# A decayed-attention and two-layer kernel on one core: the opening's running state summed in PSUM, longer warming matmuls, and a new order of the opening

## Chip, core and metric

One core of a Trainium2 chip runs the whole kernel. The metric is device time in microseconds, from the median of three runs. Engines are called as in the profile: PE (TensorE matmuls), PEld (its weight loads), DVE (VectorE), ACT (ScalarE), POOL (GpSimd), SP (SyncE, which issues the DMAs).

## What is computed

Decayed linear attention without a softmax, over 4 sequences of 576 positions with 8 heads of 64, and then two feed-forward layers with different activations, all in float32 and to float32 accuracy:

```python
scores = scale * np.matmul(q, k.transpose(0, 1, 3, 2))
Dmat = np.where(rel >= 0, gamma[:, None, None] ** rel[None, :, :], 0.0)
x = np.matmul(scores * Dmat[None], v)              # -> (2304, 512), heads side by side
h = x @ w_in;   x = (h * np.cos(h)) @ w_out        # 512 -> 2048 -> 512
h = x @ w2_in;  out = np.where(h >= 1, h, np.where(h <= -1, 0, (h + 1)**2 / 4)) @ w2_out
```

The decay is a power of a constant per head, so that attention can go chunk by chunk: within a chunk by masked scores, and across chunks by a running state, a 64x64 matrix per head, which is multiplied by the head's decay over the chunk and gets the sum of k times v of the chunk added.

## The kernel before

**Layout.** The 2304 positions are cut into blocks of 256, 512, 512, 512 and 512 for the first layer (`BLOCKS`), and the sequences into chunks of 128 or 64 that don't cross a block. Chunks 0 to 10 belong to the first three blocks (chunk 4 is the last of the first sequence, 9 the last of the second, 10 begins the third; 4 and 6 have 64 positions). A float32 operand of a large matmul is split into a high and a low part, and three matmuls make a product. A weight comes as float64 and is converted to such a pair by five steps on ACT and DVE, named X, C, W, O and M; the layer's input weight c is wi c, the output weight wo c. Converted wi tiles are also stored to DRAM for the later blocks. From c = 4 on a raw weight is loaded twice, into `raw` and `rsh`.

**A chunk's steps.** `load:qk`, `load:kv`; `q` and `k` scale q and k by tables of decay powers, on the engine that the letter behind them names (V DVE, G POOL, A ACT); `scores`; `masked` (two products with the mask table, on DVE); `state`, the matmuls of k with v; `add_state`, which makes the new state T; `across` and `attend`, the matmuls with the old state T and with the masked scores; `high` and `low`, which split the result for the first layer. `copied` copies the result out of PSUM first; then low runs on POOL instead of DVE. The `state` of every chunk goes to fresh PSUM banks y2 and y3 (`start` on its first matmuls). `add_state` (lines 374 to 386) then makes T: for a sequence's first chunk two copies on ACT, else four DVE operations of 64 columns each, old T times a decay plus the banks. The decays are columns 12 to 19 of `ktb`, a table of 20 columns, and k's are columns 0 to 11.

**First layer.** A slot is a block and an inner column tile c of 128. Its steps are m (12 matmuls, first product), h, a, A, b, C, g, G (copy and activation on ACT, DVE, POOL) and M (12 matmuls, second product). m:0 and m:1 belong to block 0 with wi0 and wi1, m:2 to block 1 with wi0, m:3 to block 0 with wi2, m:4 to block 1 with wi1, m:5 to block 0 with wi3, m:7 with wi4.

**Order.** The opening, attention for chunks 0 to 10, the first conversions and slots 0 to 7, is written out by hand: `OPENING` (lines 64 to 81) is a list of steps, `take` issues them, and what an engine gets stands in that order on it, the DMA issues of SP among them. Behind it the loop over slots goes on with the same step functions, and a scheduler orders the rest. `load_raw` of the remaining weights follows the list, so on SP they stand behind the list's last store, that of wi4. Steps `warm:n` are matmuls of a zero tile `wz` into a PSUM tile that nobody reads:

```python
wz = const.tile([P, P], BF16, tag="wz", name="wz")
m = PE.matmul(wt[:, 0:P], wz, wz, start=True, stop=True)
warm(20)
```

Of the kernel before, what the change touches and what calls it, by code (L numbers as in the profile page):

```python
# [63 lines left out]
OPENING = """
load:kv0 load:kt load:qk0 load:qt load:qk1 load:mt load:kv1 load:qk2 load:wi0 load:kv2 load:qk3 load:kv3 load:qk4
load:wo0 load:qk5 load:kv4 load:kv5 load:wi1 load:kv6 load:qk6 k:0V state:0 add_state:0 q:0V warm:5 scores:0 q:1V
warm:1 scores:1 masked:0 across:1 masked:1 attend:0 k:1G load:qk7 load:kv7 attend:1 high:0 q:2G low:0 state:1 copied:1
load:qk8 load:kv8 add_state:1 scores:2 X:wi0 high:1 W:wi0 across:2 k:2V O:wi0 C:wi0 warm:4 state:2 q:3V k:3A
add_state:2 low:1 warm:4 scores:3 masked:2 across:3 q:4G masked:3 X:wo0 warm:1 state:3 attend:2 M:wi0 store:0
load:qk10 attend:3 q:5G add_state:3 high:2 load:qk9 load:wi2 load:kv9 load:kv10 load:wo1 low:2 m:0 copied:3 W:wo0 k:5A  # L70
scores:4 C:wo0 scores:5 across:4 X:wi1 masked:4 k:6G state:5 masked:5 attend:4 add_state:5 q:6G high:4 state:6 C:wi1
attend:5 O:wo0 high:3 low:4 q:7G high:5 add_state:6 warm:1 scores:6 across:6 h:0 low:3 low:5 a:0 k:7A masked:6 warm:2
scores:7 A:0 M:wo0 across:7 attend:6 load:wi3 masked:7 q:8G high:6 state:7 k:8A low:6 attend:7 q:10G add_state:7
scores:8 W:wi1 high:7 state:8 M:wi1 across:8 O:wi1 store:1 load:wo2 low:7 q:9G b:0 warm:1 m:1 add_state:8 X:wi2 C:0
scores:9 h:1 C:wi2 g:0 across:9 a:1 m:2 A:1 W:wi2 b:1 masked:9 k:10G O:wi2 X:wo1 masked:8 G:0 state:10 h:2 attend:9
a:2 C:1 M:wi2 store:2 g:1 load:wi4 attend:8 high:9 W:wo1 X:wi3 m:3 G:1 low:9 add_state:10 W:wi3 O:wo1 m:4 h:3 C:wo1
a:3 O:wi3 C:wi3 high:8 A:2 M:0 h:4 low:8 b:2 A:3 scores:10 M:wo1 b:3 load:wo3 C:2 M:1 a:4 C:3 g:2 A:4 X:wo2 M:wi3
store:3 b:4 G:2 masked:10 m:5 g:3 C:4 attend:10 h:5 G:3 a:5 g:4 m:6 A:5 high:10 C:wo2 b:5 G:4 low:10 X:wi4 M:2 h:6 C:5
a:6 W:wo2 M:wo2 O:wo2 A:6 X:wo3 M:3 W:wi4 b:6 W:wo3 O:wi4 M:4 C:6 O:wo3 C:wi4 g:6 M:wi4 store:4 g:5 C:wo3 m:7 M:wo3
G:5 h:7 a:7 G:6 M:5 A:7 M:6 b:7 C:7 g:7 G:7  # L80
"""
# [949 lines left out]
```

## Time and profile before

| | |
|---|---|
| time, median of 3 runs | 861.61 us (859.78 to 862.84) |
| the profiled execution's own time | 860.27 us |
| its span | 858.5 us |
| PE busy | 834.2 us (97%), 5719 matmuls |
| DVE busy | 582.5 us (68%) |
| ACT busy | 443.4 us (52%) |
| POOL busy | 137.5 us (16%) |

The profiled execution took 1.34 us less than the median. The span is what the trace covers; 1.8 us lie around it. Busy times are of the whole span. The stages differ: attention and the opening up to about 80 us, conversion of the first layer's weights beside its matmuls up to about 160, and then matmuls alone. Times in the rows are counted from the span's start. A group's line number is that of a helper (L102) for everything in the opening.

### The profile page before, as it was taken

The numbers are of one execution on the slowest core, as the hardware profiler recorded it, in microseconds if no ns is written. First come the engines' busy times: TensorE is split into PE (matmuls) and PEld (weight loads), VectorE is DVE, ScalarE is ACT, GpSimd is POOL, SyncE is SP. The second block draws the span as 40 slices with busy tenths as digits, with TensorE's granted clock in tenths as the row PEclk, the third lists the DMA queues.
The fourth block names the chain that finished last, engine by engine and source line by source line (L and its number), as shares of the span: only waits on it lengthen the run. The fifth ranks groups of instructions, "written<-read, shape, count | busy, mean of one in ns | idle before, by whom it ended". The sixth has DMA issues, their size and how long they took to land.

```text
span 858.5 us, 15034 instructions
## 1 busy us (share of the span) xinstructions
PE 834.2 (97%) x5719; PEld 719.5 (84%) x5719; DVE 582.5 (68%) x1095; ACT 443.4 (52%) x859; POOL 137.5 (16%) x113
## 2 busy tenths in 40 slices
PE   6799999999999999999999999999999999999997
PEld 5688888888877888888888898988898998898986
DVE  5797887848775879687893567666554756554554
ACT  3576777755655555556665434434333444333333
POOL 2412222443223332222223000000000000000000
PEclk9899999999999999999999999999999999999999
DMA  9845999956858786778967777765765855756431
GB/s 365 331 173 189 343 357 332 350 195 229 283 182 301 292 333 226 253 244 300 316 223 244 272 240 224 280 198 181 246 193 175 268 186 174 262 177 182 137 99 73
DMA packets 67960, 206.65 MB, mean 241 GB/s; under 512 B 7472, under 2 KB 11056, under 8 KB 67888
## 3 DMA queue, kind: packets, MB, share of 16 engines
q1 hardware_dynamic: 67888, 205.69, 70.2%
q8 instruction: 45, 0.74, 0.4%
q14 instruction: 27, 0.22, 0.1%
HBM read 164.77 MB, written 40.89 MB: 240 GB/s over the span
## 4 chain that ended last, share of the span: by engine, by line
PE 89%; DVE 4%; DMA 3%; ACT 2%; issue 1%; SPq 0%; ACTq 0%; DVEq 0%
PE hq L646 20%; PE h L498 15%; PE bky L513 6%; PE bky L514 6%; PE bky L515 6%; PE bky L699 5%; PE bky L698 5%; PE bky L700 5%; PE h L102 4%; PE bky L102 3%; PE bkS L357 1%; PE bkO L698 1%; PE bkO L498 1%; PE bkS L498 1%; PE bkO L700 1%; PE bkS L699 1%
## 5 line engine op out<-in xcount | busy, mean ns | idle before, releaser
L646 PE MATMUL hq<-xc,wq 128*128 128x384 f32 x1008 | 198.7, 337 | 0.6 <-DVE sC L654 0.3
L646 PEld LDWEIGHTS hq<-xc,wq 128*128 128x128 f32 x1008 | 180.1, 188 | 12.7 <-DVE sC L654 0.6
L498 PE MATMUL h<-xhl,wi 128*128 128x512 f32 (+1 forms) x576 | 138.0, 388 | 1.5 <-ACT wi L102 1.5
L498 PEld LDWEIGHTS h<-xhl,wi 128*128 128x128 f32 x576 | 105.8, 188 | 24.1 <-ACT wi L102 1.7
L680 ACT ACTIVATE t<-t,half 128x384 f32<-128x384 f32 x96 | 58.9, 615 | 106.7 <-DVE t L679 106.6
L571 POOL TENSOR_TENSOR gl<-t,gh 128x512 fp32r<-128x512 f32 (+1 forms) x57 | 78.6, 1379 | 199.8 <-ACT gh L566 150.2
L513 PE MATMUL bky<-gh,wo 128*128 128x512 f32 x216 | 84.8, 393 | 0.0
L514 PE MATMUL bky<-gh,wo 128*128 128x512 f32 x216 | 84.3, 390 | 0.0
L515 PE MATMUL bky<-gl,wo 128*128 128x512 f32 x216 | 81.4, 390 | 0.0
L698 PE MATMUL bky<-wo,gh 128*128 128x512 f32 x192 | 75.5, 393 | 0.2 <-ACT gh L576 0.2
L699 PE MATMUL bky<-wo,gh 128*128 128x512 f32 x192 | 75.5, 393 | 0.0
L681 DVE TENSOR_TENSOR t<-t,sC 128x384 f32<-128x384 f32 x96 | 53.3, 556 | 32.1 <-ACT t L680 31.9
L576 ACT ACTIVATE gh<-t 128x384 fp32r<-128x384 f32 x96 | 50.0, 522 | 35.6 <-DVE t L681 35.1
L577 DVE TENSOR_TENSOR gl<-t,gh 128x384 fp32r<-128x384 f32 x96 | 53.0, 553 | 17.9 <-ACT gh L576 17.7
L679 DVE TENSOR_SCALAR t<-sC 128x384 f32<-128x384 f32 x96 | 34.4, 358 | 42.2 <-ACT sC L666 40.6
L700 PE MATMUL bky<-wo,gl 128*128 128x512 f32 x192 | 61.1, 394 | 0.0
L566 ACT ACTIVATE gh<-t 128x512 fp32r<-128x512 f32 (+1 forms) x57 | 35.3, 619 | 43.0 <-DVE t L559 42.9
L102 PE MATMUL h<-xhl,wi 128*128 128x256 f32 (+1 forms) x288 | 51.8, 331 | 3.5 <-DVE C L102 1.9
L554 ACT ACTIVATE t<-t 128x512 f32<-128x512 f32 (+1 forms) x56 | 34.9, 623 | 36.7 <-DVE t L550 36.5
L102 PEld LDWEIGHTS h<-xhl,wi 128*128 128x128 f32 x288 | 43.1, 189 | 10.0 <-DVE C L102 2.1
L550 DVE SCALAR_TENSOR_TENSOR t<-t,h 128x512 f32<-128x512 f32 x40 | 27.3, 683 | 31.5 <-ACT t L546 31.1
L513 PEld LDWEIGHTS bky<-gh,wo 128*128 128x128 f32 x216 | 40.5, 188 | 8.9 <-issue 0.3
(188 smaller groups left out, 1543.6 us busy)
## 6 DMA issues: line engine op xcount, KB each, us to landing
wq<-wq SPq DMA_DIRECT2D x72, 512.0 KB, 4.1
wi<-wd SPq DMA_DIRECT2D x48, 512.0 KB, 4.8
wo<-wd SPq DMA_DIRECT2D x48, 512.0 KB, 4.4
raw<-in_win_dram SPq DMA_DIRECT2D x32, 512.0 KB, 6.2
raw<-in_wout_dram SPq DMA_DIRECT2D x32, 512.0 KB, 5.8
qkv<-in_kv_dram SPq DMA_DIRECT2D x16, 512.0 KB, 8.7
...
```

The costliest lines, as they stand in the source:

```text
L102: ins = fn(*args, **kw)
L498: lastpe[0] = PE.matmul(hp[s][:, :n], w[:, a, kb, :], x[b][:, kb, :], start=(i == 0), stop=(i == 3 * KB - 1))
L513: PE.matmul(o, w[:, 0, es], a, start=first and e % per == 0, stop=False, skip_group_check=True)
L514: PE.matmul(o, w[:, 1, es], a, start=False, stop=False, skip_group_check=True)
L515: PE.matmul(o, w[:, 0, es], b, start=False, stop=last, skip_group_check=True)
L571: G.tensor_tensor(out=gl[s], in0=u, in1=f(gh[s]), op=ALU.subtract)
L646: lastmm[0] = PE.matmul(o, w[:, a, kb, :], x[b][:, kb, :], start=first and i == 0, stop=i == 5, skip_group_check=True)
L680: A.activation(t, t, AF.Square, scale=0.5, bias=half)
L681: V.tensor_tensor(out=t, in0=t, in1=h, op=ALU.max)
L698: PE.matmul(y, a[:, js], w[:, 0, :], start=n == 0, stop=False)
L699: PE.matmul(y, a[:, js], w[:, 1, :], start=False, stop=False)
L700: PE.matmul(y, b[:, js], w[:, 0, :], start=False, stop=n == NC - 1)
```

## The change

- **State.** `state` writes all chunks of the opening into the same two banks y2 and y3, which are taken once. `start` stands on the first chunk of a sequence alone, so the products of later chunks add up in PSUM. For that k is scaled relative to the end of the sequence, not of the chunk, and the new step `T` (`sum_state`) multiplies the sum by a decay to give T: on DVE two operations of 128 columns, on ACT four of 64. Nothing is added to the old T. `ktb` gets 12 columns more for each of the nine chunks that need it: 128 columns.
- **Warming.** `wz` has 512 columns and lies in a weight's home; a warming matmul has 512 columns instead of 128. At the start there are 9 instead of 20; in the list the steps are 2, 1, 1, 1, 1 instead of 5, 1, 4, 4, 1, 1, 2, 1.
- **Order.** The list is another one: other places for nearly all steps, other engines for q and k, `copied` for chunks 0, 1, 2, 4, 7 and 8 instead of 1 and 3.

```diff
 OPENING = """
-load:kv0 load:kt load:qk0 load:qt load:qk1 load:mt load:kv1 load:qk2 load:wi0 load:kv2 load:qk3 load:kv3 load:qk4
...
+load:qt load:qk0 load:mt load:kt load:kv0 load:qk1 load:kv1 load:qk2 load:wi0 load:kv2 load:qk3 load:kv3 load:wo0
...
         def decay_k(self, eng):
             k, u = self.kv[:, 0], self.n // D * 4
-            t = ktb[:, 0:8] if self.n == P else ktb[:, 8:12]
+            m0 = SUMS.get(self.i, 0 if self.n == P else 8)
+            t = ktb[:, m0:m0 + u]
...
-        def state(self, banks=None):
-
-            self.Y = [t[:, P:2 * P] for t in self.Z] if banks is None else [bank(t)[:, :P] for t in banks]
-            own = banks is not None
+        def state(self, sums=None):
+
+            own = sums is not None
+            self.Y = sums if own else [t[:, P:2 * P] for t in self.Z]
...
-                            self.mm(self.Y[r][j * D:(j + 1) * D, c * D:(c + 1) * D], self.kv[rs, 0, g], self.kv[rs, 1, g], own and c == i == 0)
+                            self.mm(self.Y[r][j * D:(j + 1) * D, c * D:(c + 1) * D], self.kv[rs, 0, g], self.kv[rs, 1, g], own and self.first and c == i == 0)
...
+        def sum_state(self, eng):
+
+            T = self.new_state()
+            m0 = SUMS[self.i] + 8
+            for r in range(2):
+                if eng is V:
+                    V.tensor_tensor(out=T[:, r].rearrange("p (c d) -> p c d", c=2), in0=self.Y[r].rearrange("p (c d) -> p c d", c=2),
+                                    in1=ktb[:, m0 + 2 * r:m0 + 2 * r + 2].unsqueeze(2).to_broadcast([P, 2, D]), op=ALU.mult)
+                    continue
+                for c in range(2):
+                    A.activation(T[:, r, c * D:(c + 1) * D], self.Y[r][:, c * D:(c + 1) * D], AF.Copy, scale=ktb[:, m0 + 2 * r + c:m0 + 2 * r + c + 1])
...
-    wz = const.tile([P, P], BF16, tag="wz", name="wz")
+    wz = wp.tile([P, 512], BF16, tag="wo5", name="wz")
...
-            m = PE.matmul(wt[:, 0:P], wz, wz, start=True, stop=True)
+            m = PE.matmul(wt, wz[:, :P], wz, start=True, stop=True)
...
-    warm(20)
+    warm(9)
...
-            chunk(int(x)).state(("y2", "y3"))
+            if not sums:
+                sums.extend(bank(t)[:, :P] for t in ("y2", "y3"))
+            chunk(int(x)).state(sums)
+        elif op == "T":
+            chunk(int(x)).sum_state(eng)
```

How the instructions stand, first on SP, whose first issues are the loads of the first chunks (`qkv` is a chunk's q and k or k and v, `qtb`, `ktb`, `mtb` the tables). Before:

```order
L102 DMA qkv<-in_kv_dram 128x1024
L102 DMA ktb<-in_ktab_dram 128x20
L102 DMA qkv<-in_qk_dram 128x1024
L102 DMA qtb<-in_qtab_dram 128x512
L102 DMA qkv<-in_qk_dram 128x1024
L102 DMA mtb<-in_mtab_dram 128x768
L102 DMA qkv<-in_kv_dram 128x1024
```

SP after the change, the same place:

```order
L104 DMA qtb<-in_qtab_dram 128x512
L104 DMA qkv<-in_qk_dram 128x1024
L104 DMA mtb<-in_mtab_dram 128x768
L104 DMA ktb<-in_ktab_dram 128x128
L104 DMA qkv<-in_kv_dram 128x1024
L104 DMA qkv<-in_qk_dram 128x1024
```

The q and k of chunk 0 with the table for q and the mask table now come ahead of its k and v, and of the table for k.

On PE the step m:1 (`h<-xhl,wi` of 256 columns; `bkO`, `bkS` and `bky` are attention's banks). Before, it stands behind chunk 8's across and a warming matmul, with the scores of chunk 9 behind it:

```order
L102 MATMUL bky_818<-qkv,T 64x128
L102 LDWEIGHTS wz
L102 MATMUL wt<-wz 128x128
L102 MATMUL h<-xhl,wi 128x256 x12
L102 MATMUL bkO<-qkv 64x128 x2
L102 MATMUL bkS<-qkv 64x128 x2
```

After, m:1 stands on PE between the attends of chunks 5 and 4:

```order
L104 MATMUL bkS<-R,qkv 64x64
L104 MATMUL bkO<-R,qkv 64x64
L104 MATMUL h<-xhl,wi 128x256 x12
L104 MATMUL bky_536<-R,qkv 64x64
L104 MATMUL bky_537<-R,qkv 64x64
```

The step moved forward, past the attends of chunks 4, 6 and 7 and the scores and states of chunks 6, 7 and 8.

And m:2 (512 columns), on PE, after the change, between chunk 7's across and its state:

```order
L104 MATMUL bkO<-qkv,T 64x128
L104 MATMUL bkS<-qkv,T 64x128
L104 MATMUL h<-xhl,wi 128x512 x12
L104 MATMUL bky_223<-qkv 64x64 x2
L104 MATMUL bky_224<-qkv 64x64 x2
```

Before, m:2 stood behind chunk 9's across. The state's banks have the numbers 223 and 224 for all chunks of the opening now.

On DVE, the new state of chunk 2 and what stands around it. Before:

```order
L102 TENSOR_TENSOR qkv<-qkv,qtb 128x512
L102 SCALAR_TENSOR_TENSOR T<-T,ktb,bky_382 128x64 x2
L102 SCALAR_TENSOR_TENSOR T<-T,ktb,bky_383 128x64 x2
L102 TENSOR_TENSOR R<-bky_345,mtb 128x384
L102 TENSOR_TENSOR R<-bky_344,mtb 128x384
```

DVE after the change:

```order
L104 SCALAR_TENSOR_TENSOR wi<-C,X 128x512
L104 TENSOR_TENSOR qkv<-qkv,ktb 128x512
L104 TENSOR_TENSOR T<-bky_223,ktb 128x128
L104 TENSOR_TENSOR T<-bky_224,ktb 128x128
L104 TENSOR_TENSOR R<-bky_337,mtb 128x384
L104 TENSOR_TENSOR R<-bky_336,mtb 128x384
```

Four operations became two, and the last step of wi0's conversion now stands ahead of the state; before, it stood behind the four mask products.

## Rows read from the trace of the kernel before

**Rows 1.** Windows by stage, us: each engine's busy time (instructions), granted clock, DMA share, GB/s.

```profile
0.00:9.29 9.29, 5.87 (x94) 4.99 (x95) 2.46 (x7) 1.93 (x4) 0.20 (x4) 1.00 0.78 298
9.29:43.12 33.83, 24.21 (x764) 21.51 (x763) 25.28 (x66) 17.90 (x61) 14.33 (x13) 0.90 0.90 360
43.12:79.78 36.66, 35.26 (x407) 30.41 (x407) 32.18 (x64) 26.41 (x60) 8.06 (x8) 1.00 0.46 161
79.78:97.29 17.51, 16.83 (x98) 14.71 (x96) 14.03 (x28) 14.66 (x31) 2.18 (x2) 1.00 0.99 358
97.29:160.00 62.71, 60.33 (x352) 52.78 (x353) 52.01 (x93) 48.87 (x105) 17.74 (x15) 1.00 0.94 335
160.00:858.50 698.50, 691.68 (x4014) 595.14 (x4012) 456.59 (x842) 333.61 (x603) 95.00 (x71) 1.00 0.68 227
```

The columns after the window and its length are PE, PEld, DVE, ACT and POOL.

**Rows 2.** Waits of PE, 9.29 to 43.12: us in total, times, longest.

```profile
PE bky L102 <- issue: 5.7, 4, 3.4
PE h L102 <- DVE C L102: 1.9, 1, 1.9
```

**Rows 3.** Timeline of PE: start, us, instructions, idle time before and what ended it.

```profile
33.61 0.38 PE L102 MATMUL bky<-qkv 64*64 64x64 f32 x4 [3.41 <-issue]
```

**Rows 4.** Windows as in rows 1, cut where PE resumes.

```profile
9.29:14.77 5.48, 4.49 (x132) 4.22 (x131) 2.64 (x6) 1.92 (x6) 2.32 (x2) 1.00 1.03 419
14.77:20.91 6.14, 3.92 (x128) 3.25 (x128) 5.65 (x15) 3.65 (x11) 2.25 (x3) 1.00 1.03 414
20.91:26.92 6.01, 4.15 (x136) 3.64 (x128) 5.94 (x15) 3.61 (x13) 3.08 (x4) 1.00 1.03 412
26.92:33.61 6.69, 3.14 (x125) 2.77 (x126) 4.08 (x9) 2.08 (x7) 2.67 (x3) 0.92 1.02 402
33.61:39.49 5.88, 5.72 (x127) 4.98 (x127) 3.69 (x12) 3.26 (x12) 4.01 (x4) 0.51 0.89 359
39.49:43.12 3.63, 2.79 (x126) 2.65 (x125) 3.28 (x12) 3.38 (x14) 0.00 (x0) 1.00 0.04 14
```

**Rows 5.** DMA view, 0 to 45 us: queue, transfers, MB, share of 16 engines.

```profile
q8 instruction: 6, 0.10, 0.8%
```

**Rows 6.** Chain of waits, 40 to 160 us: start, us, what (m:1, m:2).

```profile
43.96 1.48 PE h L102 x12
46.49 2.96 PE h L102 x12
```

**Rows 7.** Timeline of PE: the first warming matmuls, and two states of 32 matmuls.

```profile
1.02 2.32 PE L766 MATMUL wt<-wz 128*128 128x128 bf16 x20 [1.02 <-DVE wz L761]
5.30 1.14 PE L102 MATMUL bky<-qkv 64*64 64x64 f32 x32 [1.96 <-DVE qkv L102]
18.02 0.69 PE L102 MATMUL bky<-qkv 64*64 64x64 f32 x32 [1.15 <-issue]
```

**Rows 8.** Timeline of DVE, 0 to 10 us.

```profile
4.55 0.69 DVE L102 TENSOR_TENSOR qkv<-qkv,ktb 128x512 f32<-128x512 f32 x1 [2.20 <-DMA ktb<-in_ktab_dram]
6.78 0.69 DVE L102 TENSOR_TENSOR qkv<-qkv,qtb 128x512 f32<-128x512 f32 x1 [1.53 <-DMA qtb<-in_qtab_dram]
8.12 0.69 DVE L102 TENSOR_TENSOR qkv<-qkv,qtb 128x512 f32<-128x512 f32 x1 [0.65 <-DMA qkv<-in_qk_dram]
9.13 1.02 DVE L102 TENSOR_TENSOR R<-bky,mtb 128x384 f32<-128x384 f32 x2 [0.32 <-PE bky L102]
```

**Rows 9.** Timeline of POOL: the first scaling of a k.

```profile
10.40 1.04 POOL L102 TENSOR_TENSOR qkv<-qkv,ktb 128x512 f32<-128x512 f32 x1 [9.96 <-DMA qkv<-in_kv_dram]
```

**Rows 10.** Groups of DVE, 0 to 45 us: busy us, mean ns, idle before.

```profile
L102 DVE SCALAR_TENSOR_TENSOR T<-T,ktb,bky 128x64 f32<-128x64 f32 x24 | 5.1, 273 | 4.1 <-PE bky L102 4.0
L102 DVE TENSOR_TENSOR R<-bky,mtb 128x128 f32<-128x128 f32 x4 | 1.0, 284 | 0.7 <-PE bky L102 0.7
```

**Rows 11.** Chain of waits, 40 to 160 us: start, us, what.

```profile
73.43 5.74 DMA rsh<-in_win_dram
...
97.29 2.12 PE bky L102 x8
```

More of the change, by code (lines that the diff above doesn't have):

```diff
@@ L61 @@
 NCH = len(CHUNKS)
+OPEN = [i for i, (b, t, n) in enumerate(CHUNKS) if _block_of(b * S + t) <= 2]
+SUMS = {i: 20 + 12 * j for j, i in enumerate(i for i in OPEN if CHUNKS[i][1] + CHUNKS[i][2] < S)}
+KT = 20 + 12 * len(SUMS)
 OPENING = """
-load:kv0 load:kt load:qk0 load:qt load:qk1 load:mt load:kv1 load:qk2 load:wi0 load:kv2 load:qk3 load:kv3 load:qk4
-load:wo0 load:qk5 load:kv4 load:kv5 load:wi1 load:kv6 load:qk6 k:0V state:0 add_state:0 q:0V warm:5 scores:0 q:1V
-warm:1 scores:1 masked:0 across:1 masked:1 attend:0 k:1G load:qk7 load:kv7 attend:1 high:0 q:2G low:0 state:1 copied:1
@@ L68 @@
[L68 to L77, printed above, removed]
@@ L78 @@
-store:3 b:4 G:2 masked:10 m:5 g:3 C:4 attend:10 h:5 G:3 a:5 g:4 m:6 A:5 high:10 C:wo2 b:5 G:4 low:10 X:wi4 M:2 h:6 C:5
-a:6 W:wo2 M:wo2 O:wo2 A:6 X:wo3 M:3 W:wi4 b:6 W:wo3 O:wi4 M:4 C:6 O:wo3 C:wi4 g:6 M:wi4 store:4 g:5 C:wo3 m:7 M:wo3
-G:5 h:7 a:7 G:6 M:5 A:7 M:6 b:7 C:7 g:7 G:7
+load:qt load:qk0 load:mt load:kt load:kv0 load:qk1 load:kv1 load:qk2 load:wi0 load:kv2 load:qk3 load:kv3 load:wo0
+load:qk4 load:kv5 load:kv4 load:qk5 load:kv6 load:wi1 q:0V scores:0 masked:0 k:0G warm:2 attend:0 q:1G state:0
@@ new lines @@
+copied:0 load:qk7 load:qk6 load:kv7 T:0V high:0 k:1V warm:1 scores:1 low:0 across:1 state:1 masked:1 q:2G T:1V warm:1
+attend:1 X:wi0 C:wi0 k:2A scores:2 W:wi0 across:2 q:3V M:wi0 copied:1 warm:1 state:2 k:3V high:1 scores:3 O:wi0
+store:0 T:2V low:1 masked:2 X:wo0 across:3 state:3 q:4G masked:3 W:wo0 attend:3 k:5V O:wo0 C:wo0 attend:2 high:3 k:6A
+load:kv10 load:qk10 load:qk8 load:kv8 load:qk9 load:wi2 load:wo1 load:kv9 M:wo0 m:0 load:wi3 low:3 q:5G copied:2 T:3V
+high:2 scores:4 C:wi1 X:wi1 h:0 W:wi1 a:0 q:6V O:wi1 scores:5 q:7V k:7A across:4 state:5 masked:5 low:2 warm:1
@@ new lines @@
+attend:5 M:wi1 store:1 load:wo2 A:0 m:1 high:5 masked:4 k:10G b:0 low:5 attend:4 h:1 q:10V a:1 C:0 q:8V g:0 scores:7
+copied:4 G:0 T:5V high:4 scores:6 k:8V across:6 state:6 masked:6 T:6A q:9G attend:6 high:6 across:7 A:1 X:wi2 C:wi2
+b:1 low:4 low:6 X:wo1 W:wi2 m:2 M:wi2 O:wi2 store:2 load:wi4 W:wo1 X:wi3 masked:7 O:wo1 state:7 h:2 C:wo1 attend:7 a:2
+T:7V scores:8 copied:7 A:2 state:8 high:7 C:wi3 across:8 b:2 scores:9 masked:8 low:7 m:3 T:8A C:2 attend:8 h:3 W:wi3
+g:2 across:9 m:4 copied:8 masked:9 G:2 O:wi3 a:3 M:wo1 high:8 load:wo3 A:3 X:wo2 C:1 scores:10 M:wi3 store:3 b:3
@@ L446, in x @@
         def x(self):
-            if self.off == 0 and self.blk not in xhl:
+            if self.blk not in xhl:
                 new_x(self.blk, BLOCKS[self.blk][1])
```

28 lines of the change are left out of this document (21 added, 7 removed).

## Prediction

> **What bounds the kernel now.** I read the stages first. From 160 us to the end PE is busy 691.68 of 698.50 us; before that the five stages leave it idle for 3.42, 9.62, 1.40, 0.68 and 2.38 us [rows 1]. The change touches the opening alone, and what stands behind it keeps PE full, so the time can move only by as much earlier or later as PE gets through the opening.
>
> The largest loss is the stage from 9.29 to 43.12. The waits of PE there are mostly put down to "issue": 5.7 us in 4 waits, for nothing that semaphores explain [rows 2]. The longest is 3.41 us and ends at 33.61, in the middle of one chunk's state matmuls, whose operands were there [rows 3]. What it is shows in the counts. Cut at the points where PE resumes, the stage falls into six pieces, and each holds 251 to 264 matmuls and weight loads together [rows 4]; the DMA view has a queue named instruction with six transfers, 0.10 MB together, up to 45 us [rows 5]. So I read: PE's program comes in blocks of 256 instructions, and PE stops at the end of a block until the next has come. While the other transfers fill the DMA engines (share 1.02 to 1.03) a block takes 5.48 to 6.69 us; the fifth, at a share of 0.89, takes 5.88; the sixth, at 0.04, takes 3.63 [rows 4]. PE was busy only 3.14 to 4.49 us of each of the first four. In the fifth it was busy 5.72 of 5.88, but at a granted clock of 0.51, the 1.2 GHz level, into which it had fallen during the 3.41 us. So up to 43.12 this stage is as long as its six fetches, 33.83 us, and hardly as what the matmuls cost.
>
> The Trainium skill, "Runtime: NRT & Kernel Launch", Instruction fetch mechanics, also has blocks of 256 instructions, but calls the crossing "mostly hidden". By that sentence the issue waits have another cause; the third rival below is what this would give. The trace speaks against it, since a wait stood at the end of nearly every block.
>
> **The change, part by part.**
> *Warming matmuls.* Before 43.12 the old order has 38 of them, the new one 15 up to the same point in the work: 23 fewer, and with a weight load each 46 instructions fewer. I counted in order's rows (a 64-row float32 matmul there is two matmuls and two weight loads in the trace). In both kernels the sixth piece ends in or just behind the state of chunk 8. The old kernel has then done one first-layer step, m:0. The new one has done m:0, m:1 and m:2: their 48 instructions stand where the 46 stood. These two take 1.48 and 2.96 us on the chain of waits, just behind 43.12 [rows 6]. If the new kernel also gets through its six blocks in 33.83 us, it has **4.44 us** less to do behind them. The longer warming matmuls (512 columns) cost no fetch; the 4 in this stretch take at most four times the 116 ns of a 128-column one at the low clock (20 in 2.32 us [rows 7]), 1.9 us in a stage with 9.62 us of idle: nothing, covered by the fetch. Without that cover it is 1.9 us.
>
> *The start.* The first boundary passes at 9.29 in the old kernel, in the second scores; in the new order it lies in the middle of the first chunk's state. The old loads let DVE begin at 4.55 with 0.53 MB in, at 6.78 with 1.32 MB and at 8.12 with 1.84 MB [rows 8]. Interpolated, q of chunk 0 (now 0.79 MB in) starts at 5.3 instead of 6.78, and the first kv (1.77 MB in), the first to come before, is there at 7.9. k:0 on POOL takes 1.04 us [rows 9], so state:0 starts at 9.0 at the earliest and the boundary in its middle is at 9.3. The other branch, q (0.69), scores (as the matmuls of the old first scores, 1.4 times the state's 1.14 us), mask (1.02 [rows 8]) and attend (as long as the scores), gives 10.2, and a boundary at 10.7, if all runs at the low clock. That PE is there at first in the old kernel is seen from a state of 32 matmuls: 1.14 us at 5.30, 0.69 us at 18.02 [rows 7]. The 9 long matmuls keep PE at work from about 1 to about 5 us, where 20 short ones ended at 3.34 [rows 7]; I take the clock as up by 7, and the boundary at 9.7: **0.4 us late**, bounds 0 and 1.4. The table of 64 KB in place of 10 KB is in the sum of bytes.
>
> *State in PSUM.* The old update is four DVE operations of 273 ns mean, 24 in 5.1 us on end [rows 10]: 0.85 us each time. The new one is two of 128x128 from PSUM; the nearest row is the mask product of that size, 284 ns [rows 10], so 0.57 us, bounds 0.4 and 0.85. Six of the nine run so on DVE, as many as before, and three on ACT, in place of three plain copies. Saved on DVE: 1.7 us over the opening, bounds 0 and 2.7. PE's next state has to wait for the read of the bank, as it did, so no wait goes or comes. The new order also gives DVE four more scalings of q and k (0.69 us each [rows 8]) and takes four low parts from it, about the same, which go by ACT and POOL. In the second stage all this is worth nothing, the fetch is later; behind it DVE is busy 32.18 of 36.66 us [rows 1], and there it counts only through the next part.
>
> *Order of conversions.* From 43.12 to 79.78 PE waits 1.40 us [rows 1], for weight conversions in the main. In the new order the fourth wi conversion stands seven rows earlier on DVE, wo0 and wi1 far earlier, in the time in which DVE idled 8.55 us of the second stage [rows 1]. But PE asks for the fourth wi earlier too, by the 4 us. I take 1.0 us of waits in place of 1.40, bounds 0 and 3: **0.4 us** gained. Then SP: the weight loads behind the list wait for the fifth wi to be stored; on the chain the first of them, issued at 73.43, takes 5.74 us, and from there conversions and one more such transfer lead to PE at 97.29 [rows 11], behind the 0.68 us wait of that stage. With the fifth wi earlier these move with it: **0.4** of the 0.68. The last 2.38 us up to 160 [rows 1] I leave as they are, 1 either way.
>
> *Sum*: 4.44 - 0.4 + 0.4 + 0.4 = 4.8 us. The profiled execution took 860.27 us, so 855.5; the median of the three is 861.61, 1.3 more, so 856.8 by that. I put the forecast between, at **856.2** (that is 861.0 less 4.8), with a range of its own from 853 to 858.5.
>
> **The rivals.**
> *The clock falls once in a fetch wait.* In each of the first four blocks the new kernel has no more to do than the old one, so waits of about 2 us stand at their ends; one of 3.41 us [rows 3] was enough to bring the clock to 0.51 in the next piece, one of 1.9 [rows 2] was not. Where m:1 or m:2 falls into such a stretch, each us of matmuls becomes two. A stretch as long as the fifth and a little of the fourth piece, 6.7 us, costs at most half of it, 3.4: 859.6. The Trainium skill, "TensorE: Matmul & The Clock Gate", HAM oscillation, tells of waits between bursts of matmuls that bring the low clock back each time; the trace shows one.
> *Slower: the low clock stays.* If the 8 fewer warming matmuls of the stretch leave PE so idle that it stays at 1.2 GHz from 9 to 34 us, the first four blocks need twice 15.7 us (their busy time) in 24.3 [rows 4]: 7.1 over, and 1.5 more for m:1, less 4.8: 3.8 slower, 864.8. It decides from the point where a block's work at the low clock is longer than its fetch, that is 3 us at the full one. For it: fewer warming matmuls, a wait in each block. Against: those left are four times as long, and a PE that worked on without pause was back at the full clock in the sixth piece.
> *The fetch is not the pace.* Then the waits stay where they are in time, the matmuls that went had stood in idle time, and only the small terms are left, 0.8: 860.2.
> *Conversions late.* DVE or its loads bind at m:5 and m:7 with the bound of 3 us: 858.2.
> *More.* Fetches are asked for in emptier moments, or the waits between 43 and 160 go too: 4 us more, 852.
>
> **How the numbers follow.** Chances: forecast 0.40, clock once 0.17, slower 0.10, no pace 0.10, conversions 0.13, more 0.10. A measurement of this kernel can tell about 0.3%, 2.6 us, from no change, so faster is below 859.0 and slower above 864.2. Faster: 0.40, 0.10 for more, 0.10 of the conversions, 0.06 of the clock: 0.66. Slower: 0.10. Same: 0.24. The range from 851.5 to 862.5 leaves out the slower case and a part of "more".
>
> **What would show it.** Right: pieces of 256 instructions of 5.5 to 6.7 us up to about 38, waits named issue at their ends, the sixth piece ending at 43 to 44.5 with m:1 and m:2 done, and the step m:8, which opens the stage at 79.78, at 74 to 76. Wrong start: the first boundary after 10.7. Wrong clock: a granted clock of 0.5 over a stretch with m:1 or m:2 in it. Wrong conversions: waits of PE for wi or wo of over 2 us between 45 and 75. If the blocks come in under 5 us while the DMA engines are full, the fetch is not what I take it for.

## Result: 8.5 us faster, and the profile after

| | before | after |
|---|---|---|
| time, median | 862.1 us (5 runs, 859.78 to 862.84) | 853.33 us (5 runs, 852.13 to 854.58) |
| ratio, 95% interval | | 0.9901, 0.9882 to 0.9920 |
| profiled execution: time, span | 860.27, 858.5 us | 853.70, 851.9 us |

The forecast was 856.2 us, 4.8 us less than before. The sign was right; the gain is 8.5 us by the ratio (7 to 10), nearly twice the 4.8. The two profiled executions differ by 6.57 us. The one of before was itself about 1.8 us faster than the median; what is known of this spread stands at the end of the part on the prediction.

The stages of the changed kernel, which answer to [rows 1] (window, its length, then busy time and instructions of PE, PEld, DVE, ACT, POOL, then granted clock, DMA share, GB/s):

```profile
0.00:9.40 9.40, 6.30 (x92) 3.14 (x96) 2.10 (x6) 1.94 (x4) 1.36 (x6) 1.00 0.80 295
9.40:46.12 36.72, 27.31 (x774) 23.93 (x773) 32.37 (x69) 23.25 (x66) 13.39 (x11) 0.91 0.96 376
46.12:76.34 30.22, 30.22 (x393) 26.67 (x385) 25.52 (x50) 23.93 (x56) 10.03 (x9) 1.00 0.51 178
76.34:160.00 83.66, 81.85 (x478) 72.20 (x477) 67.33 (x123) 65.92 (x141) 21.97 (x19) 1.00 0.96 344
160.00:851.90 691.90, 686.20 (x3985) 590.59 (x3983) 453.57 (x834) 328.59 (x593) 91.97 (x69) 1.00 0.68 225
```

The cuts are at the same points of the work as before: the first block boundary, the sixth boundary behind it, and m:8. The second stage is 2.9 us longer than the 33.83 us of [rows 1]. The third is 6.44 us shorter and leaves PE idle for nothing, where 1.40 us of waits had been. Cut at the boundaries, as in [rows 4]:

```profile
9.40:15.48 6.08, 3.11 (x141) 2.89 (x135) 4.67 (x11) 1.53 (x3) 4.12 (x3) 1.00 1.02 413
15.48:21.55 6.07, 3.85 (x128) 3.12 (x129) 4.52 (x10) 4.40 (x13) 1.98 (x2) 1.00 1.04 403
21.55:27.62 6.07, 6.02 (x128) 5.63 (x129) 5.84 (x13) 4.02 (x12) 1.85 (x2) 0.72 1.03 404
27.62:35.47 7.85, 5.62 (x126) 5.30 (x130) 7.82 (x15) 4.58 (x16) 2.61 (x2) 0.78 1.01 401
35.47:42.88 7.41, 6.12 (x140) 4.53 (x137) 6.31 (x16) 6.12 (x18) 2.83 (x3) 1.00 0.96 352
42.88:46.12 3.24, 2.60 (x127) 2.46 (x129) 3.21 (x8) 2.60 (x7) 0.00 (x0) 1.00 0.48 193
```

Three pieces of 256 instructions take 6.07 or 6.08 us each, though PE's work in them differs from 3.11 to 6.02 us. The fourth and fifth are longer than any before. The waits of PE in this stage (us in total, times, longest) say why; against [rows 2], DVE stands first and "issue" second:

```profile
PE bkS L104 <- DVE R L104: 3.5, 3, 2.2
PE bky L104 <- issue: 2.9, 2, 1.5
PE bkO L104 <- POOL qkv L104: 0.8, 1, 0.8
PE h L104 <- DVE xhl L104: 0.5, 1, 0.5
```

Three rows of PE's timeline (start, us, what, idle before): the end of the 2.23 us wait for the masked scores of chunk 5 (R), m:1, and m:8.

```profile
31.33 0.32 PE L104 MATMUL bkS<-R,qkv 64*64 64x128 f32 x1 [2.23 <-DVE R L104]
...
32.50 2.86 PE L104 MATMUL h<-xhl,wi 128*128 128x256 f32 x12
...
76.34 4.32 PE L104 MATMUL h<-xhl,wi 128*128 128x512 f32 x24
```

DVE was busy 7.82 of the 7.85 us of the fourth piece: that wait is DVE's load. m:1 took 2.86 us because the clock had fallen. It fell twice, each time to 0.50 for about 3.4 us, where [rows 4] show one fall with 0.51 over 5.88 us:

```profile
21.50:24.90 3.40, 3.36 (x85) 3.36 (x89) 3.30 (x6) 1.33 (x4) 1.32 (x1) 0.50 1.03 404
31.73:35.15 3.42, 3.42 (x40) 3.28 (x32) 3.42 (x9) 1.38 (x4) 1.04 (x1) 0.50 1.02 406
```

Behind m:8 a second gain stands. Windows that hold 192 matmuls of 512 and 228 of 256 columns each, the same work in another order, before, after, and (third) the new order alone, an experiment below:

```profile
92.30:167.92 75.62, 72.56 (x421) 63.34 (x420) 62.59 (x113) 59.35 (x126) 20.19 (x17) 1.00 0.94 336
```

```profile
90.54:162.68 72.14, 71.45 (x422) 63.35 (x420) 60.94 (x110) 58.47 (x127) 19.97 (x17) 1.00 0.96 345
```

```profile
94.20:166.22 72.02, 71.45 (x421) 63.34 (x420) 60.60 (x110) 58.54 (x127) 20.94 (x17) 1.00 0.97 347
```

The same work takes 3.48 us less. The waits of PE in the windows, before:

```profile
PE h L498 <- ACT wi L102: 1.5, 1, 1.5
PE h L102 <- ACT wi L102: 0.8, 1, 0.8
PE bky L102 <- ACT gh L102: 0.7, 1, 0.7
```

and after:

```profile
PE h L104 <- ACT wi L104: 0.7, 1, 0.7
```

So 3.0 us of waits for weight conversions and activations on ACT became 0.7. The waits' rows cover 2.3 of the 3.48 us; the rest is in shorter gaps between the matmuls.

The change edits the list of the opening alone, but it does not leave the rest as it was. From the 26th matmul on, counted from the start of m:8, PE has another order of instructions, and so have ACT and DVE from m:8 on. It is one order in before and the three experiments with the old list, and another in the kernels with the new list (but for a_store_late, below). The scheduler that orders the rest comes to another result behind another opening.

### The profile page after: what moved, and what is told of

Same layout as the page of the kernel before. It is cut to its first block, busy times and chain, and to the rows that moved or that the text cites. A ratio compares the mean times of both kernels' runs of the same rounds, so it can differ in the third digit from the quotient of the medians.

```text
span 851.9 us, 14957 instructions
## 1 busy us (share of the span) xinstructions
PE 831.9 (98%) x5691; PEld 716.5 (84%) x5695; DVE 580.9 (68%) x1080; ACT 443.6 (52%) x857; POOL 138.7 (16%) x113
## 4 chain that ended last, share of the span: by engine, by line
PE 86%; DVE 6%; DMA 4%; ACT 3%; issue 1%; SPq 0%; ACTq 0%; DVEq 0%
PE hq L666 20%; PE h L518 15%; PE bky L533 6%; PE bky L534 6%; PE bky L535 6%; PE bky L719 5%; PE bky L718 5%; PE bky L720 5%; PE h L104 2%; PE bky L104 1%; PE bkS L360 1%; PE bkO L720 1%; PE bkS L719 1%; PE bkO L718 1%; PE bkO L518 1%; PE bkS L518 1%
## 5 line engine op out<-in xcount | busy, mean ns | idle before, releaser
L104 PE MATMUL h<-xhl,wi 128*128 128x256 f32 (+1 forms) x288 | 54.1, 336 | 2.2 <-ACT hs L104 1.0
L535 PEld LDWEIGHTS bky<-gl,wo 128*128 128x128 f32 x216 | 40.5, 188 | 8.5
```

Source lines behind the costliest of these rows:

```text
L104: ins = fn(*args, **kw)
L535: PE.matmul(o, w[:, 0, es], b, start=False, stop=last, skip_group_check=True)
```

## Experiments

All ratios are to the kernel before, on the same chip. A quick way to read the profiles of all of them is by three distances: the first boundary, from there to m:8, and from m:8 to the end of the span. (Boundaries are where the count of PE's matmuls and weight loads passes 193 and every 256 from there; of PE's 54 issue waits up to 50 us in these profiles, 48 stand at them. The fifth and the sixth boundary below are counted behind the first.)

| kernel | ratio, 95% interval | first boundary | to m:8 | to the end |
|---|---|---|---|---|
| before | 1 | 9.29 | 70.5 | 778.7 |
| b_sum | 0.9993 (0.9984 to 1.0002) | 10.88 | 70.9 | 778.7 |
| b_warm | 0.9972 (0.9962 to 0.9983) | 10.93 | 68.7 | 778.2 |
| b_start | 1.0008 (0.9996 to 1.0019) | 9.47 | 70.5 | 780.5 |
| a_order | 0.9938 (0.9921 to 0.9955) | 9.81 | 71.8 | 773.9 |
| a_oldwarm | 0.9905 (0.9892 to 0.9919) | 10.08 | 68.6 | 774.7 |
| a_addstate | 0.9913 (0.9900 to 0.9927) | 9.96 | 67.0 | 775.1 |
| after | 0.9901 (0.9882 to 0.9920) | 9.40 | 66.9 | 775.6 |
| a_m_late | 0.9972 (0.9960 to 0.9984) | 9.53 | 72.4 | 774.7 |
| a_tiny | 0.9944 (0.9932 to 0.9956) | 10.59 | 69.1 | 775.3 |
| a_dummy | 0.9902 (0.9889 to 0.9915) | 9.96 | 66.8 | 774.5 |
| a_store_late | 0.9913 (0.9900 to 0.9926) | 9.81 | 65.6 | 778.1 |
| a_mask5 | 0.9896 (0.9878 to 0.9914) | 9.83 | 66.1 | 775.3 |
| a_best | 0.9896 (0.9875 to 0.9917) | 10.37 | 66.2 | 774.5 |

### One part alone, on the kernel before

**The sum in PSUM (b_sum).** New `state`, `sum_state`, tables; in the old list:

```diff
-add_state:0 ... add_state:1 ... add_state:5 ...
+T:0A ... T:1V ... T:5A ...          (0, 5, 10 on ACT, the others on DVE)
```

> The kernel before with one part of the change alone: the opening's state is summed in PSUM and scaled on the way out (six on DVE, three on ACT); order and warming are the old ones. PE's instructions are the same in number and in place. Fetch theory (PE's pace up to 43 us is that of its instruction blocks): the first four block boundaries stay within 0.3 us of 9.29, 14.77, 20.91, 26.92, and the time moves by 0, at most -0.8 us for the DVE work that is gone behind 43 us. Rival, the new sum itself brings the gain: DVE saves 1.7 us over the opening and PE waited for DVE, so -1.7 us or more. A loss: the next state in the same two banks has to wait for the read of the sum, up to +1 us.

861.56 us: no difference that can be measured, and the gain of 1.7 us is out. The boundaries came 1.0 to 1.6 us later than expected: q of chunk 0 started on DVE at 8.36 and not at 6.78 [rows 8], since its load came later in this execution. The longer table ahead of it (64 KB in place of 10) is at most a small part of that, since b_warm below, with the short table, has 8.21.

```profile
8.36 0.69 DVE L106 TENSOR_TENSOR qkv<-qkv,qtb 128x512 f32<-128x512 f32 x1 [3.02 <-DMA qtb<-in_qtab_dram]
```

The table shows that the rest went as before from there.

**The warming alone (b_warm).**

```diff
-    warm(20)
+    warm(9)
-... warm:5 ... warm:1 ... warm:4 ... warm:4 ... warm:1 ... warm:1 ... warm:2 ... warm:1
+... warm:2 ...            warm:2 ... warm:1 ...                       warm:1 ... warm:1
```

> The kernel before with one part of the change alone: warming matmuls of 512 columns, 9 at the start and 2, 2, 1, 1, 1, 1 in the list at old places, so 23 matmuls and 46 PE instructions fewer ahead of the state of chunk 8; order and state are the old ones. Fetch theory: block boundaries stay where they were in time (9.3, 14.8, 20.9, 26.9) and the work stands 46 instructions further at each; behind 43 us m:1 and the first scores of chunk 9 have moved into the blocks, so -1.1 us (46 x 6.07/256) at the least and -2.5 at the most. Rival, the order does it: the matmuls that went stood in idle time, so 0 within 0.5 us. Clock theory: the full clock comes about 7 us earlier than at 12.03, first boundary at 8.3 or earlier.

859.39 us, 2.4 less (1.5 to 3.3). That the matmuls went for nothing is out; the fetch theory's 1.1 to 2.5 fits. The boundaries did not stay in time, as that theory had them: q came late here too, and the first was at 10.93. Measured from it, the next three stand at 4.95, 11.90 and 17.43 us, against 5.48, 11.62 and 17.63 before. The clock theory's first boundary of 8.3 was not put to a fair test: the granted clock was full early (a state of 32 matmuls at 5.33 took 0.69 us), but while PE waited 2.39 us for the late q it fell, to 0.50 from 8 to 14.8. From the first boundary to m:8 b_warm needs 1.8 us less than before, 2.2 less than b_sum. Second to fourth piece:

```profile
15.88:22.83 6.95, 4.32 (x126) 3.34 (x128) 6.84 (x16) 4.24 (x12) 3.40 (x3) 0.91 1.03 414
22.83:28.36 5.53, 5.36 (x140) 5.02 (x134) 5.05 (x12) 2.80 (x11) 2.50 (x4) 0.80 1.03 414
28.36:34.22 5.86, 2.85 (x126) 2.44 (x127) 4.92 (x14) 2.92 (x9) 2.21 (x3) 1.00 1.02 412
```

The pieces are about as long as in [rows 4], with other work in them.

**The start alone (b_start).**

```diff
-load:kv0 load:kt load:qk0 load:qt load:qk1 load:mt load:kv1 ... k:0V state:0 add_state:0 q:0V warm:5 scores:0
+load:qt load:qk0 load:mt load:kt load:kv0 load:qk1 load:kv1 ... q:0V warm:5 scores:0 masked:0 k:0G warm:1 attend:0
```

> The kernel before with the start of the new order alone: the table for q, q and k of chunk 0, and the mask table are loaded ahead of the table for k and of k and v, and scores, mask and attend of chunk 0 stand ahead of its state; all behind chunk 1's scores as before. Theory, later work follows the first block boundary: where the old start lets it pass between 9.3 and 10.9, as its three profiles show, and the new one between 9.4 and 10.6, the median moves by 0 to -1.0 us. Rival, the prediction's term (0.4 us late, bounds 0 and 1.4): 0 to +1.4 us.

862.23 us, ratio 1.0008: the start brings nothing, and a gain of 1 us is out. The prediction's 0.4 us late is inside the interval.

**The order alone (a_order).** The new list, with the old `add_state` and old warming:

```diff
-warm(9) ... warm:2 ... warm:1 ... warm:1 ... warm:1 ... warm:1 ... T:0V ... T:6A
+warm(20) ... warm:6 ... warm:3 ... warm:3 ... warm:3 ... warm:3 ... add_state:0 ... add_state:6
```

> The kernel before with one part of the change alone: the new order, with the state in fresh banks and the old update on DVE, and with warming matmuls of 128 columns, 20 at the start and 18 in the list. Theory, the order is nearly all of it, because it puts m:1 and m:2 and the conversions where PE waits for instructions or for DVE anyway: the two parts taken back one at a time cost 0.9 and 0.2 us, so -7.4 us against before, within 1.5. Rival, the prediction's step: the 46 instructions must go for m:1 and m:2 to find room, so at least 1.1 us and up to 4.4 on top of the 0.9 for the state: -6.5 to -3.2 us.

Ratio 0.9938, so 5.3 us less (3.9 to 6.8). It is the largest part, but not nearly all of it: it fell into the range that the prediction's step gives, though the interval reaches into the other. The table shows where its gain is: 4.8 us behind m:8, and none ahead of it (71.8 against 70.5). Ahead of m:8, m:2 stands past the fifth boundary here, and PE waits there:

```profile
42.75 0.28 PE L104 MATMUL bky<-R,qkv 64*64 64x64 f32 x3 [2.27 <-issue]
```

Taken alone, the three parts have -0.6 us (not clear of zero), -2.4 and -5.3: -8.3 together, near the 8.5.

### One part taken back, on the changed kernel

**The old state (a_addstate)** and **the old warming (a_oldwarm).**

```diff
-T:0V ... T:1V ... T:2V ... T:6A           (a_addstate: fresh banks, old ktb)
+add_state:0 ... add_state:1 ... add_state:2 ... add_state:6
```

> The changed kernel with one part taken back: each chunk's state goes to fresh banks, and T is made of the old T and the new banks, by four DVE operations of 64 columns (two copies on ACT for a first chunk). Order and warming stay the new ones. Fetch theory: the first three boundaries stay within 0.3 us of 9.40, 15.48, 21.55; where PE waits for DVE (2.23 us before 31.33) two updates more stand ahead on DVE, 0.57 us, and from 35 us on three more that were on ACT: +0.5 to +1.5 us in all. Rival, the sum is what brings the gain: +3 us or more.

```diff
-    warm(9)                               (a_oldwarm: 128 columns again)
+    warm(20)
-warm:2 ... warm:1 ... warm:1 ... warm:1 ... warm:1
+warm:6 ... warm:3 ... warm:3 ... warm:3 ... warm:3
```

> The changed kernel with one part taken back: warming matmuls of 128 columns, 20 at the start and 6, 3, 3, 3, 3 in the list, so 23 matmuls and 46 PE instructions more; order and state stay the new ones. Fetch theory: boundaries stay near 9.4, 15.5, 21.6, 27.6 and the work stands 46 instructions back at each: +1.1 us (46 x 6.07/256) at the least, up to +4.4 if a first-layer step leaves the six blocks. Rival, the order does it: 0 within 0.5 us. Clock theory: the full clock comes only at about 12 instead of 4.42, and the first boundary at 10 or later: +0.6 to +1.5 from that alone.

854.23 and 853.48 us: neither can be told from the changed kernel's 853.33 (by the ratios 1.0 and 0.3 us more, each about 2 either way). For the old warming the fetch theory had at least 1.1; its one trace does need 1.7 us more up to m:8. But both taken back at once, which is a_order, cost 3.2 us, about 2 either way (0.9938 against 0.9901). So in the new order each of the two parts makes up for the lack of the other. The traces say the same with a difference: from the first boundary to m:8, a_order needs 71.8 us, the old warming 68.6, the old state 67.0, the changed kernel 66.9. From a_order to a_addstate only the warming changes, by 46 instructions, and it gives 4.8 us there, between one execution of each; the time by the ratios shows 2.2, about 2 either way. From a_order to a_oldwarm only the state changes, and 3.2 us go: a_oldwarm too has m:2 past the fifth boundary, but PE waits there 0.27 us and not 2.27, and m:2 takes 3.25 us and not 4.45, since in a_order the clock had fallen (0.76 in that piece). Why the fifth block came so late in a_order was not found.

**m:1 and m:2 late (a_m_late).**

```diff
-A:0 m:1 high:5 ... h:1 ... a:1 ... W:wi2 m:2 M:wi2 ... state:7 h:2 ... copied:7 A:2 state:8 high:7
+A:0 high:5 ... W:wi2 M:wi2 ... state:7 ... copied:7 state:8 m:1 h:1 a:1 high:7 C:wi3 m:2 h:2 A:1 a:2 b:1 A:2
```

> The changed kernel with m:1 and m:2 (and the steps behind them, h, a, A, b) moved back behind the state of chunk 8, where they stood before; everything else as in the changed kernel. Fetch theory: up to the sixth boundary PE goes at the pace of its blocks, whatever lies in them, so the fourth to sixth pieces (7.85, 7.41, 3.24 us) become about 6.1, 6.1 and 3.6, the sixth boundary comes at 43.4 instead of 46.12, and m:1 and m:2 are paid behind it at the full clock with 4.44 us: 4.44 - 2.7 = +1.7 us, up to +3.5 where a piece stays long. Rival, what the new order gains is conversions and DVE work that come earlier, not the place of these two steps: 0 within 0.5 us.

859.63 us, 6.1 us more than the changed kernel by the ratios, about 2 either way, and 5.5 us more from the first boundary to m:8: most of the gain. That the place of the two steps doesn't matter is out, and the 1.7 to 3.5 us was too little. Up to the fifth boundary it went as expected, pieces of 6.51 and 5.86 us. In the fifth piece, behind waits for DVE, the clock was already down (0.56). Then PE stands without work of its own in front of DVE, and the clock goes down again (0.80):

```profile
34.19:40.05 5.86, 5.06 (x138) 4.55 (x135) 5.60 (x14) 3.66 (x12) 3.17 (x3) 0.56 1.03 405
40.05:48.55 8.50, 5.75 (x128) 5.50 (x127) 5.43 (x13) 2.48 (x5) 0.00 (x0) 0.80 0.79 291
```

```profile
43.19 0.47 PE L104 MATMUL bkS<-R,qkv 64*64 64x128 f32 x1 [2.75 <-DVE R L104]
```

In the changed kernel m:1 and m:2 lie in this time. So they use waits for instructions and waits for DVE alike, and keep PE at work besides. (Their ACT and DVE steps moved with them, which this run does not tell apart.)

### Is it the fetch?

**The fetches in the traces.** The queue named instruction (q8) moves one packet of 16 KB per piece, and the traces have its times. In the fourteen profiles up to 50 us each of the 48 issue waits at a boundary ended 1.20 to 1.62 us after such a packet had landed. In the kernel before, packets landed at 13.28, 32.17, 38.27 and 41.71, and PE went on at 14.77, 33.61, 39.49 and 43.12. The packet itself takes 0.9 to 1.3 us. What changes is when it starts: 3.05 to 4.28 us behind the boundary before it in the first five pieces of before, 1.24 us in the sixth, with the engines nearly empty.

In the changed kernel the packets landed at 13.98, 20.24 and 26.30 for the boundaries at 15.48, 21.55 and 27.62, which fits the same distance, but at 32.99, 39.46 and 43.19 for those at 35.47, 42.88 and 46.12. In these last three PE came later than its instructions.

**64 matmuls that nobody needs (a_tiny).**

```diff
-across:1 state:1 masked:1
+across:1 state:1 tiny:64 masked:1
+            PE.matmul(wt[:, :16], wz[:, :P], wz[:, :16], start=True, stop=True)
```

> The changed kernel with 64 more warming matmuls of 16 columns behind the state of chunk 1, at about 16 us: 128 PE instructions, half a block, that nobody waits for. Fetch theory: the second and third boundaries stay within 0.4 us of 15.48 and 21.55, as measured from the first, with the work half a block back; the time goes up by 1.6 us (half of the sixth piece of 3.24) to 3.0 us (128 x 6.07/256). Rival, PE waits in that stretch for operands and not for instructions: the 64 run in the idle time (1.39 us before 21.54 and some small waits) and the time moves by 0 to +0.6 us.

857.20 us, 3.7 more than the changed kernel (0.9944 against 0.9901), about 2 either way, and 2.2 more from the first boundary to m:8. The rival had at most 0.6; the theory's 3.0 lies within the interval. Measured from the first boundary, the second and third came at 5.48 and 11.60 us, where 6.08 and 12.15 within 0.4 were expected: 0.6 early. The 64 cost PE little of its own time: 41 of them in a row take 1.18 us. But a boundary now lies among them, and PE waits there, with nothing to wait for but instructions:

```profile
13.42 1.18 PE L104 MATMUL wt<-wz 128*128 128x16 bf16 x41
16.07 0.95 PE L104 MATMUL wt<-wz 128*128 128x16 bf16 x24 [1.47 <-issue]
...
22.19 0.43 PE L104 MATMUL bky<-qkv 64*64 64x64 f32 x10 [2.41 <-issue]
```

The second and third pieces took 6.12 and 6.29. SP's next load, k and v of chunk 10, went out at 29.61 instead of 25.54, and the DMA engines ran empty for a while. (Some of the 3.7 us may come from these later loads.) That gave a test that was not planned, the third and fourth piece:

```profile
22.19:28.48 6.29, 4.48 (x128) 4.04 (x127) 5.41 (x12) 2.23 (x7) 1.27 (x1) 0.73 0.95 374
28.48:32.51 4.03, 4.02 (x125) 3.83 (x129) 3.24 (x8) 2.54 (x6) 1.28 (x1) 1.00 0.46 143
```

At a DMA share of 0.46 the next block was there in 4.03 us or less, since PE was busy 4.02 of them; its packet started 1.15 us behind the boundary.

**More transfers at the sixth piece (a_dummy).**

```diff
-A:0 m:1 high:5
+A:0 m:1 dummy:5 high:5
+                SY.dma_start(out=dummy[:, k], in_=kv[k][:, :])
```

> The changed kernel with five more transfers of 512 KB from DRAM to DRAM, that nobody reads, issued by SP behind the load of wo2, so that the DMA engines stay full for about 7 us longer than to 44.3. Fetch theory: pieces of 256 instructions whose fetch falls into that time take the 6.07 us of the first three: the sixth takes 5.5 us or more instead of 3.24, and the time goes up by 2 to 4 us. Rival, a piece is as long as PE's work: the sixth stays at 3.2 to 3.6 us, and the time moves only by what the later loads and stores (the store of wi2, the load of wi4) cost, 0 to +1 us.

853.47 us, as the changed kernel. The sixth piece took 4.96 us, at a DMA share of 1.03, with an issue wait at its end:

```profile
41.50:46.46 4.96, 3.61 (x130) 2.93 (x128) 4.86 (x12) 3.95 (x8) 0.27 (x1) 1.00 1.03 412
```

```profile
46.46 0.39 PE L104 MATMUL bky<-qkv 64*64 64x64 f32 x10 [0.70 <-issue]
```

That lies between the two expectations, 5.5 or more and 3.2 to 3.6, and in a_best the piece took 4.42 us without the transfers. The 2 to 4 us of time did not come (0.1 by the ratios, about 2 either way). The direction fits the fetch: the packet, which started at 42.06 in the changed kernel, ahead of the boundary, starts here 2.65 us behind it and lands at 45.08. The size is inconclusive.

**Loads later (a_store_late).**

```diff
-store:4 C:wo3
+store:4 hold:wo2 C:wo3       (hold: a DMA of 8 KB out of wo2's converted tile)
```

> The changed kernel with one small transfer more on SP behind the store of wi4, that waits for the end of the conversion of wo2; so the weight loads behind the list, issued from 65.58 on, are issued from about 72.4 on, nearly where they stood before (72.88). Theory, that these earlier loads took the waits of PE between 76 and 160 us away (before 2.96 us in three, now 1.80): they come back, +1.0 to +1.5 us. Rival, the waits come from the order that the scheduler gives to the rest: 0 within 0.5 us.

The edit failed to do what it was for: the conversion of wo2 was done when SP came to the transfer, and the loads went out at 65.08, no later than 65.58 in the changed kernel. So whether the earlier loads took the waits behind m:8 away was not tested. The 854.79 us can't be told from the changed kernel. The edit also changed the order that the scheduler gives to the rest: from the 148th matmul on, counted from the start of m:8, it is a third one. The profile shows what one wait can cost; PE, and the windows behind it:

```profile
136.72 2.93 PE L104 MATMUL h<-xhl,wi 128*128 128x256 f32 x12 [2.01 <-ACT wi L104]
```

```profile
136.72:138.72 2.00, 2.00 (x9) 2.00 (x10) 1.93 (x5) 1.29 (x3) 1.07 (x1) 0.50 1.13 281
138.72:140.72 2.00, 2.00 (x10) 1.77 (x9) 1.16 (x2) 0.80 (x2) 1.64 (x2) 0.66 0.67 246
```

Twelve matmuls take 2.93 us at the low clock. In the 778.1 us behind m:8 in the table are this wait and this clock.

### Take the DVE wait away

**a_mask5** and **a_best.** Both put the masks of chunk 5 earlier on DVE; a_best also moves two DVE operations back.

```diff
-a:0 q:6V O:wi1 scores:5 q:7V k:7A across:4 state:5 masked:5 low:2
+a:0 scores:5 k:7A across:4 state:5 masked:5 q:6V O:wi1 q:7V low:2      (both)
-load:kv9 M:wo0 m:0 ... h:1 q:10V a:1 ... k:8V across:6 ... masked:7 O:wo1
+load:kv9 m:0 ... h:1 a:1 ... k:8V M:wo0 across:6 ... masked:7 q:10V O:wo1   (a_best)
```

> The changed kernel with the mask products of chunk 5 two operations earlier on DVE, ahead of the scaling of q of chunks 6 and 7, to shorten the 2.21 us in which PE waits for them before 31.33. Theory, PE's pace from 28 to 43 is set by DVE's work as a whole: the wait shrinks by about 1 us, but later waits for q and for the masks of chunks 6 and 7 grow by as much, so 0 within 0.8 us. Rival, that wait is the bound: -1.0 to -1.4 us, and up to 1.3 more if m:1 then runs at the full clock.

> As the run with the mask products of chunk 5 earlier, and two more DVE operations later: the last step of wo0's conversion (1.65 us at 23.76) goes behind the scaling of k of chunk 8, where DVE idles for 0.96 us, and the scaling of q of chunk 10 (0.68 us) goes behind the masks of chunk 7. Theory, DVE's work between 24 and 37 paces PE there: 2.3 us less of it ahead of the masks give -1 to -2 us, as far as the instruction blocks (about 6.1 us each) let PE follow. Rival, the blocks set the pace there and not DVE: 0 within 0.8 us.

853.07 and 852.81 us: no difference to the changed kernel that can be measured (0.4 less by the ratios, 2.4 either way, so the times alone leave room for both expectations), though the edits did what they were for. In a_best the wait before chunk 5's attend is 0.20 instead of 2.23 us, the clock stays at 1.00 from the first boundary at 10.37 on, and m:1 takes 1.70 instead of 2.86. The waits of PE there, beside those of the changed kernel above:

```profile
PE bky L104 <- issue: 4.0, 3, 2.2
PE bkO L104 <- issue: 1.8, 1, 1.8
PE bky L104 <- DVE R L104: 1.7, 3, 1.1
PE bkS L104 <- DVE R L104: 1.2, 3, 0.6
```

Issue rose from 2.9 to 5.8 us. Of that, 0.8 stands at 22.02, ahead of the place of the edits; 2.3 is new behind it, 1.76 at 28.22 and 0.54 at 34.32, where the packets had landed at 26.80 and 32.95. Second to fifth piece:

```profile
15.91:22.02 6.11, 3.69 (x127) 2.88 (x127) 5.40 (x13) 4.70 (x14) 1.97 (x2) 1.00 1.04 402
22.02:28.22 6.20, 4.43 (x127) 4.04 (x128) 4.86 (x11) 4.14 (x12) 2.55 (x2) 1.00 1.03 406
28.22:34.32 6.10, 4.84 (x128) 4.00 (x129) 5.54 (x13) 4.41 (x15) 1.26 (x1) 1.00 1.02 411
34.32:41.38 7.06, 5.08 (x127) 3.93 (x126) 6.96 (x15) 5.20 (x16) 3.08 (x3) 1.00 1.03 404
```

PE has less to do in them at the full clock, and still they take 6.1 to 6.2 us, three in a row. For the rival that the blocks set the pace this is the best sign: a wait was taken away, and a wait for instructions stood in its place.

## Why the prediction was right, and where its sizes were wrong

**The pace by blocks** held for the first three pieces of the changed kernel, not for the last three. In all fourteen profiles the second and third pieces, with the DMA engines full, took 5.40 to 6.95 us, whatever PE had to do in them; instructions that were added cost 3.7 us, taken away they gave 2.4 us (b_warm), a DVE wait that was shortened became an issue wait; and the packets show the fetch itself. The sign against it, blocks under 5 us with the engines full, did turn up: 4.84, 4.95 and 4.86 us for the first pieces of b_sum, b_warm and a_oldwarm, 4.96 for the sixth of a_dummy. There the packets started 2.36 to 2.71 us behind the boundary, and PE went on 1.3 to 1.4 us after they had landed, as elsewhere. So the fetch is the pace, but "about 6 us" is no fixed price.

The rows were read a little wrongly. One of the four issue waits [rows 2], 1.15 us before 18.02 [rows 7], is not at a boundary but 114 instructions behind one: it ended 0.1 us after DVE had scaled k of chunk 2 (17.24 to 17.92). The 1.9 us put down to DVE's C [rows 2] end at a boundary, 26.92, in the middle of m:0, 1.33 us after a packet had landed: that one looks like a fetch wait. The Trainium skill, "Runtime: NRT & Kernel Launch", Instruction fetch mechanics, with its "mostly hidden", does not hold for this stage: a_tiny alone has 1.47 and 2.41 us of issue at two boundaries. The rival of that sentence, 860.2, is out.

**The 4.44 us** was the right step with a flaw in its reason. That m:1 and m:2 moved into the blocks is worth as much or more (6.1 us in a_m_late), and taking the 46 instructions out gave 4.8 us up to m:8 in the new order (a_order to a_addstate, one execution of each; 2.2 of time) as long as the state was the old one. But the exchange, 46 instructions out and 48 in, is not what it hangs on: with the state summed in PSUM the old warming did as well (a_oldwarm).

**"In the second stage all this is worth nothing, the fetch is later"** failed. I had counted DVE's work as covered by the fetch. In the fourth piece DVE was the later one, 2.23 us, and the stage became 36.72 instead of 33.83 us. The sixth boundary came at 46.12, not 43 to 44.5, m:8 at 76.34, a little behind the 74 to 76.

**The clock** rival came true in a milder form. It did fall, and m:1 lay in it, which was listed as the sign of a wrong forecast. That fall followed the wait for DVE, though, and not a fetch wait, as the rival had it. Each fall lasted about 3.4 us and not 6.7. m:1 at 2.86 against 1.70 in a_best gives a price of 1.2 us, where 3.4 was the bound. The Trainium skill, "TensorE: Matmul & The Clock Gate", HAM oscillation, has the low clock come back with the waits between bursts; the changed kernel shows two falls, a_best, with issue waits of up to 2.2 us, none.

**Start**: the boundary at 9.40 for 9.7 forecast, which is in part luck: the ten executions with the new order have 9.40 to 10.59, and this is the earliest. The start alone changed nothing that can be measured (b_start). **The new update** on DVE: 281 ns for 284 forecast.

```profile
L104 DVE TENSOR_TENSOR T<-bky,ktb 128x128 f32<-128x128 f32 x12 | 2.9, 281 | 2.2 <-PE bky L104 2.2
```

**Conversions between 43 and 80**: I took 1.0 us of waits for 1.40; there were none.

**The mis-sized term** is the last one, 0.4 us behind m:8, and with it the premise that the change touches the opening alone. From m:8 to the end the changed kernel took 775.6 us against 778.7, 3.1 less, and the table shows that it belongs to the order: the old order has 778.2 to 780.5, the new one 773.9 to 775.6, but for the one execution with the low clock. The stretch of the same 420 matmuls measured 3.48 us of it. I had followed the chain [rows 11] to one wait of 0.68 and left the 2.38 us up to 160 as they were, 1 either way. In that stretch 2.4 of these 3.06 us went (0.69 us of idle is left). Two things changed with the list: the loads behind it start 10.8 us ahead of m:8 in the changed kernel (65.58 for 76.34), 6.9 before (72.88 for 79.78); and the order of the instructions behind m:8 is another one. No run separates them. The trace of before speaks rather for the order. ACT there, ahead of PE's wait of 1.5 us:

```profile
147.94 0.38 ACT L102 ACTIVATE hs<-h 128x256 f32<-128x256 f32 x1 [2.10 <-PE h L102]
...
149.00 0.67 ACT L102 ACTIVATE X<-raw 128x512 f32<-128x512 f32 x1
...
150.38 0.63 ACT L102 ACTIVATE wi<-W 128x512 fp32r<-128x512 f32 x1
```

The raw tile, issued at 141.40, had landed at 147.5, but its conversion stood behind other steps on ACT and began at 149.00; ahead of the 0.8 us wait it had landed at 116.4 and began at 118.00. So these two waits were not directly for a load. The cause of the 3.1 us stays open.

So the account of the two profiled executions, 858.5 to 851.9: 3.44 up to m:8, where the sum had 4.4, and 3.1 behind it, where it had 0.4. The errors went against each other, so a part of the nearness is luck. The 3.1 are the 3.5 of that stretch, 1.4 late in the kernel at a wait of before that b_start alone seems to share (first row, before), less 1.7 just behind m:8, where the changed kernel waited in this execution (second row, after), and no other kernel with the new order for more than 0.22 us:

```profile
734.43 0.50 PE L698 MATMUL bkO<-wo,gh 128*128 128x512 f32 x1 [1.20 <-DVE st L521]
```

```profile
83.08 4.45 PE L104 MATMUL h<-xhl,wi 128*128 128x512 f32 x24 [1.00 <-ACT hs L104]
```

The median moved by 2 us more than this pair. The profiled execution of before had its first boundary at 9.29; b_sum and b_warm, with the same order of loads at the start, had 10.88 and 10.93. If later work follows that boundary, an early one makes up for most of the 2 us; how it is spread over the timed runs was not seen.
